# Top-k attention and two gated layers on one core: a lighter decode of layer 2's weights, new latencies in the planner, and zeros multiplied in TensorE's gaps

## The chip, the cores and the metric

The kernel runs on one core of a Trainium2 chip. The metric is device time in microseconds, from a run's start to its end; lower is better. The core has five engines that run side by side, each through its own instructions in a fixed order: TensorE (PE in the profile; PEld is its weight load), VectorE (DVE), ScalarE (ACT), GpSimd (POOL) and SyncE (SP), which here issues all transfers. Engines wait for each other by semaphores.

## The reference

```
scores = q @ k.T / sqrt(64)              # 4 batches, 8 heads, 576 rows, 64 wide
keep the 32 largest scores of a row, softmax over them
x   = attn @ v                           # 2304 tokens x 512
xn  = x / rms(x) * rms_g                 # layer 1, d_ff 1536
x   = (silu(xn @ w_gate) * (xn @ w_val)) @ w_out
out = (sigmoid(x @ w_gate2) * (x @ w_val2)) @ w_out2     # layer 2
```

The weights come in as 64-bit floats, so each value is a pair of 32-bit words (lo, hi), and the kernel turns the pair into a 32-bit float itself.

## The kernel before

The work is cut into 18 units of 128 tokens. Attention runs per unit and head: TensorE makes the scores `sp` in PSUM (two buffers), VectorE finds the 32 largest with four MAX8 and three MATCH_REPLACE8 and masks the exponentials that ScalarE made (`e`), ScalarE and GpSimd split the result into two float16 parts (`ph`), a transposing transfer turns it (`pt`), and TensorE multiplies it with the values (`pv`). Layer 1 of a unit is six products of 48 multiplications (`pg` and `pw` in three blocks) and one of 144 (`py`). Layer 2 is again six products of 48, and 36 wide multiplications (`po`). All products split their operands into two float16 parts.

Both layers' weights are prepared early. Layer 1's nine pieces (w1g, w1v, w1o, three blocks each) stay on chip; layer 2's nine pieces are decoded, scaled, split, written to DRAM (w2g, w2v, w2o) and loaded again as `wl` whenever a batch of units needs them. A piece is four blocks of 128x512. For each block `load_f32` loads the raw words (`raw`, in a ring of seven buffers that `wh` and `wl` share), and makes the float: VectorE shifts and masks the high word into `dec` in PSUM, VectorE joins the sign bits to it, ScalarE scales the low word in place, and GpSimd adds the two. `prep_piece` then finds a power of two that scales the piece, over TensorE and VectorE, and splits the blocks. `consts1` and `consts2` combine all pieces' scales; the first units of layer 1 and of layer 2 wait for them (`c1...`, `c2...`, the latter ending in the tile `c2o`).

Nothing of this is issued as written. `Scheduler` records every operation, gives it a priority (a due place in the order), and `order` walks through a planned time: it picks, again and again, the operation that can start first on some engine, with costs from `cost`. An operation's users become ready at its planned end plus a latency of its engine plus MARGIN; a transfer's users at its planned landing plus a fixed 900 ns. The order that results is the order in which each engine's instructions are written out. Planned times themselves leave no other mark on the program. PSUM tiles tagged `mm` come from one ring of three buffers; `dec`, the scale products, `pg`, `pw`, `py` and `po` share it.

Of the kernel before, what the change touches and what calls it, by code (L numbers as in the profile page):

```python
# [9 lines left out]
F32 = mybir.dt.float32  # L10
F16 = mybir.dt.float16
BF16 = mybir.dt.bfloat16
I32 = mybir.dt.int32
U32 = mybir.dt.uint32
AF = mybir.ActivationFunctionType
ALU = mybir.AluOpType
PSUM = bass.MemoryType.PSUM
DRAM = bass.MemoryType.DRAM
P = 128
# [10 lines left out]

BACKLOG = 8000
COLD = 5000.0
MARGIN = 120

ADDS = (0, 1, 2, 3)
ADDS2 = (0, 1, 2, 3)  # L40
REACH = 100.0
PATIENCE = 0.0

# [90 lines left out]
class Scheduler:  # L134
# [67 lines left out]
    def cost(self, eng, method, args, kw, writes, reads):  # L202

        out = (writes or reads)[0].shadow
        src = max([x.shadow for x in reads] + [out], key=lambda a: math.prod(a.shape[1:]))
        n = math.prod(src.shape[1:])
        psum = any(x.tile.pool.space == PSUM for x in reads + writes)
        ptrs = sum(isinstance(x, _View) for x in (*args[2:], kw.get("scalar"), kw.get("scale"), kw.get("bias")))
        if eng == "tensor":
            rate = 0.6 if method == "matmul" and kw["rhs"].shadow.dtype == F32 else 2.4  # L210
            return math.prod(out.shape[1:]) / rate + 2.7, 260
        if eng == "vector":
            if method in ("max", "match_replace", "tensor_tensor"):
                ptrs = 0
            if method == "match_replace":
                return n / 0.96 + 130, 170
            fast = method in ("tensor_scalar", "tensor_copy", "memset") and not psum
            return (8 if method == "reciprocal" else 1) * n / (1.92 if fast else 0.96) + 69 + 60 * min(ptrs, 1), 170
        if eng == "scalar":
            return n * 0.8333 + (51 if psum else 93) + 93 * (ptrs + ("accum_out" in kw)), 200  # L220
        if eng == "gpsimd":
            if method == "tensor_tensor":
                return (464 if n == 1 else n * (1.88 if mybir.dt.size(out.dtype) == 2 else 2.1) + 149), 150
            return n * 0.833 + (224 if n == 1 else 161), 150

        run = out.shape[-1] * mybir.dt.size(out.dtype)
        size = n * math.prod(out.shape[:1]) * mybir.dt.size(out.dtype)
        if method == "dma_start_transpose":
            return 1275, size / 290
        return (475 if out.shape[0] == 128 else 650), size / (360 if run >= 512 else 180)  # L230

    def order(self):
# [22 lines left out]
        now = dict.fromkeys(self.ENGINES, 0.0)  # L255
        out, dma, sems, cold = [], 0.0, [0.0] * 8, COLD

# [32 lines left out]
            return best  # L290

        behind = sorted(self.ops, key=lambda op: -op.base)
        while len(out) < len(self.ops):

            while behind[-1].end is not None:
                behind.pop()
            best = choose(behind[-1].base + REACH) or choose(math.inf)
            if best is None:
                raise RuntimeError("the schedule is stuck")
            _, at, op = best  # L300
            cost = op.cost
            if op.eng == "tensor":

                cold = COLD if at - now[op.eng] > 2500 else cold
                slow = min(cost, cold / 2)
                cold -= 2 * slow
                cost += slow
            op.start, op.end = at, at + cost
            done = op.end + op.lat + MARGIN
            if op.eng == "sync":  # L310
                move = op.calls[0][0] == "dma_start_transpose"
                begin = max(op.end + (0 if move else 650), dma)
                dma = begin + op.lat
                done = dma + 900
                sems = sems[1:] + [done]
                if move:
                    op.end = begin + 56
            now[op.eng] = op.end
            ready[op.eng].remove(op)
            out.append(op)  # L320
            for t in op.new:
                r = self.rings[t.key]
                r["free"].pop(0)
                r["lanes"][t.lane].remove(t)
            for t in op.tiles:
                t.left -= 1
                t.end = max(t.end, done)
                if not t.left:
                    r = self.rings[t.key]
                    r["free"].append(t.end)  # L330
                    r["free"].sort()

            for u in op.users:
                u.start = max(u.start, op.end + OWN if u.eng == op.eng != "sync" else done)
            for u in op.users + op.later:
                u.waits -= 1
                if not u.waits:
                    ready[u.eng].append(u)
        self.end = max(now.values())
        return out  # L340

    def issue(self):
        with self.tc.manual_schedule():
# [11 lines left out]
def topk_attention_moe_kernel(  # L355
# [17 lines left out]
    nc = E = Scheduler(tc)  # L373
# [8 lines left out]
    CPJ = 512 // P  # L382
    assert (S, D, R, DM) == (576, 64, 64, 512) and F % 512 == 0 and B % 2 == 0

    def pool(name, bufs, **kw):
        return E.pool(ctx.enter_context(tc.tile_pool(name=name, bufs=bufs, **kw)), bufs, **kw)

    const = pool("const", 1)
# [20 lines left out]
    at = pool("at", 2)  # L409
# [3 lines left out]
    htp = pool("htp", 4)  # L413
# [2 lines left out]
    ps_v = pool("ps_v", 1, space=PSUM)  # L416
    ps_m = pool("ps_m", 3, space=PSUM)
    dram = pool("dram", 1, space=DRAM)

    def pow2_scale(m, n, name, pl=None, out=None):  # L420

# [6 lines left out]
        return s.bitcast(F32), i.bitcast(F32)  # L428


    def load_f32(dst, src, on_pool):

        if src.dtype == F32:
            nc.sync.dma_start(dst, src)
            return
        raw = wbig.tile([P, 512, 2], I32, name="raw", tag="w4")
        nc.sync.dma_start(raw.rearrange("p f a -> p (f a)"), src.bitcast(I32))
        lo, hi, d = raw[:, :, 0], raw[:, :, 1], dst.bitcast(I32)

        t = ps_m.tile([P, 512], I32, name="dec", tag="mm", lane="dec")  # L440
        E.claim(dst)
        nc.vector.tensor_scalar(t, hi, 3, 0x3FFFFFF8, op0=ALU.logical_shift_left, op1=ALU.bitwise_and)
        o = d if on_pool else t
        nc.vector.scalar_tensor_tensor(
            out=o, in0=hi, scalar=-0x40000000, in1=t, op0=ALU.bitwise_and, op1=ALU.bitwise_or
        )
        if on_pool:

            nc.scalar.activation(lo, lo.bitcast(U32), AF.Copy, scale=2.0 ** -29)
            nc.gpsimd.tensor_tensor(out=d, in0=d, in1=lo, op=ALU.add)  # L450
            return
        nc.vector.scalar_tensor_tensor(
            out=d.bitcast(U32), in0=lo.bitcast(U32), scalar=29, in1=t.bitcast(U32), op0=ALU.logical_shift_right, op1=ALU.bitwise_or
        )

    def prep_piece(w, kind, j, g, s, i, place, held=None):

# [2 lines left out]
        for c in range(CPJ):  # L462
            r = (c if kind == "in" else j * CPJ + c) * P
            src = w[r : r + P, j * 512 : (j + 1) * 512] if kind == "in" else w[r : r + P, :]
            fs.append((held or place)(c).bitcast(F32))
            load_f32(fs[-1], src, c in (ADDS if held else ADDS2))

        ps = ps_m.tile([P, P], F32, name="wps", tag="mm", lane="wps")
        with E.group():
# [15 lines left out]
        else:  # L485
            nc.vector.tensor_scalar(n, m, state["g2"], 2.0 ** -30, op0=ALU.mult, op1=ALU.max)
        m = n
        pow2_scale(m, 1, "w", out=(s, i))
        sf = s.bitcast(F32)
        if g is not None:  # L490
            sc = tiny.tile([P, NC], F32, name="gsc")
            nc.gpsimd.tensor_scalar(sc, g, sf, None, op0=ALU.mult)
# [30 lines left out]
    def prep1(n, j):  # L523
        w, kind, g = {"g": (w_gate, "in", g_sb), "v": (w_val, "in", g_sb), "o": (w_out, "out", None)}[n]

        t = res[3 * j + "gvo".index(n)]
        if 3 * j + "gvo".index(n) < 3 * NJ - 1:
            held = lambda c: res[3 * j + "gvo".index(n) + 1][:, c]
        else:
            fs = [htp.tile([P, 2, CPJ, P], F16, name="fs", tag="ht2", bufs=6, lane="fs") for _ in range(CPJ)]  # L530
            held = lambda c: fs[c].rearrange("p a m r -> p (a m r)")
        pieces, s, i = lay1[n]
        prep_piece(w, kind, j, g, s[:, j : j + 1], i[:, j : j + 1], lambda c: t[:, c], held)
        pieces.append([t[:, c] for c in range(CPJ)])

    def prep2(n, j):
        w, kind = {"g": (w_gate2, "in"), "v": (w_val2, "in"), "o": (w_out2, "out")}[n]
        pieces, s, i = lay2[n]
        d = dram.tile([CPJ // 2, P, 2048], F16, name=f"w2{n}{j}")
        ts = [wbig.tile([P, 2, 1024], F16, name="wh", tag="w4") for _ in range(CPJ // 2)]  # L540
        prep_piece(w, kind, j, None, s[:, j : j + 1], i[:, j : j + 1], lambda c: ts[c // 2][:, c % 2])
        for a, t in enumerate(ts):
            nc.sync.dma_start(d[a], t.rearrange("p c f -> p (c f)"))
        pieces.append(d)
# [507 lines left out]
```

## Time and profile before

| | |
|---|---|
| median of 3 runs | 1283.01 us (1282.52 to 1285.65) |
| the profiled execution's own time | 1278.91 us |
| its span, first to last instruction | 1277.1 us |
| mean granted TensorE clock | 0.949 |
| busy: PE, DVE, ACT, POOL | 1136.7, 1021.9, 820.5, 844.6 us |

Busy times are sums over the span; one engine's share differs between stretches, so shares are read by stretch. The granted clock is 1.00 at TensorE's full speed. Every instruction carries line L351, the line at which the recorded operations are issued, so rows are told apart by tile names.

### The profile page before, as it was taken

The page shows a single profiled execution, that of the slowest core. Times are in us where ns is not written, and L with a number is a line of the kernel's source. Part 1 is how long each engine was busy: PE and PEld are TensorE (multiplying, and loading weights), DVE is VectorE, ACT ScalarE, POOL GpSimd, SP SyncE. Part 2 cuts the span into 40 slices and gives each one's busy share as a digit, 9 for nine tenths or more (in the row PEclk, how much of TensorE's full clock was granted, in tenths as well). Part 3 has the DMA queues.
Part 4 walks back from the last instruction along what each step waited for, and adds up shares of the span by engine and source line. Part 5 has one row for each costly group of instructions (what it writes and reads, how often), then busy time and mean ns, then how long its engine had stood idle before and what let it go on. Part 6 is the DMA issues. An engine that isn't in the chain of part 4 may idle for free.

```text
span 1277.1 us, 41563 instructions
## 1 busy us (share of the span) xinstructions
PE 1136.7 (89%) x17020; PEld 972.8 (76%) x17020; DVE 1021.9 (80%) x2571; ACT 820.5 (64%) x1428; POOL 844.6 (66%) x966
## 2 busy tenths in 40 slices
PE   3686364699989999999999999998999999999998
PEld 2343263698889879978896999798869978997986
DVE  6999999987888989898888899787689997980001
ACT  6898677666686757676865567566756665652531
POOL 6897889876677647685866577475747674762530
PEclk9699576799989999999999999998999999999999
DMA  8986788799877686688868577867675575765337
GB/s 283 306 253 156 246 231 225 185 282 243 127 171 158 132 185 126 135 187 184 173 140 192 118 172 136 196 127 159 137 183 118 130 168 127 175 147 138 126 106 274
DMA packets 323775, 225.26 MB, mean 176 GB/s; under 512 B 278401, under 2 KB 286593, under 8 KB 323585
## 3 DMA queue, kind: packets, MB, share of 16 engines
q1 hardware_dynamic: 323584, 222.62, 71.5%
q8 instruction: 133, 2.18, 0.7%
q14 instruction: 58, 0.47, 0.1%
HBM read 147.06 MB, written 14.16 MB: 126 GB/s over the span
## 4 chain that ended last, share of the span: by engine, by line
PE 52%; DMA 14%; DVE 8%; POOL 7%; issue 4%; ACT 4%; SPq 1%; POOLq 0%; ACTq 0%; DVEq 0%
PE pw L351 15%; PE pg L351 14%; PE po L351 9%; PE py L351 8%; DMA pt<-ph 7%; PE pv L351 3%; DMA qt<-qn 3%; DVE m L351 3%; PE sp L351 3%; DVE w L351 2%; POOL ph L351 2%; DMA xt<-sn 2%; POOL sg L351 2%; POOL wh L351 1%; SPq L351 1%
## 5 line engine op out<-in xcount | busy, mean ns | idle before, releaser
L351 DVE MAX8 m<-w 128x8 f32<-128x576 f32 x432 | 317.6, 750 | 3.1
L351 PEld LDWEIGHTS <-wl 128*128 128x128 f16 x5184 | 296.2, 99 | 2.3 <-issue 1.6
L351 POOL TENSOR_TENSOR ph<-e,ph 128x512 f16<-128x512 f32 (+1 forms) x288 | 204.5, 734 | 69.6 <-ACT ph L351 68.1
L351 DVE MATCH_REPLACE8 w<-m,w 128x576 f32<-128x576 f32 x288 | 213.3, 743 | 0.0
L351 POOL TENSOR_TENSOR sg<-sg,sv 128x512 f32<-128x512 f32 x105 | 133.9, 1276 | 44.9 <-ACT sv L351 41.1
L351 ACT ACTIVATE e<-sp,nb,sc 128x576 f32<-128x576 f32 x144 | 117.6, 829 | 69.5 <-DVE w L351 25.0
L351 PE MATMUL pg<-xt,w1g 128*128 128x128 f16 x2592 | 157.7, 222 | 4.5 <-DMA xt<-sn 4.5
L351 PE MATMUL pg<-yt,wl 128*128 128x128 f16 x2592 | 157.7, 222 | 0.9 <-POOL yt L351 0.9
L351 PEld LDWEIGHTS <-w1g 128*128 128x128 f16 (+1 forms) x2624 | 153.8, 100 | 5.0 <-issue 4.7
L351 PEld LDWEIGHTS <-w1v 128*128 128x128 f16 (+1 forms) x2640 | 150.7, 99 | 8.5 <-POOL w1v L351 5.4
L351 PE MATMUL pw<-xt,w1v 128*128 128x128 f16 x2592 | 154.7, 220 | 0.1
L351 PEld LDWEIGHTS <-w1o 128*128 128x128 f16 (+1 forms) x2640 | 150.9, 99 | 4.1 <-DVE w1g L351 3.3
L351 PE MATMUL pw<-yt,wl 128*128 128x128 f16 x2592 | 153.5, 219 | 0.4 <-DVE ym L351 0.2
L351 POOL TENSOR_TENSOR ht<-sg,ht 128x512 f16<-128x512 f32 x105 | 122.0, 1162 | 46.9 <-ACT ht L351 44.1
L351 PE MATMUL py<-ht,w1o 128*128 128x128 f16 x2592 | 150.0, 221 | 0.0
L351 PE MATMUL po<-wl,ht 128*128 128x512 f16 x648 | 145.5, 379 | 0.0
L351 DVE MAX8 m<-sp 128x8 f32<-128x576 f32 x144 | 108.2, 759 | 41.5 <-PE sp L351 40.3
L351 ACT ACTIVATE ph<-e 128x576 f16<-128x576 f32 x144 | 97.1, 677 | 51.5 <-DVE e L351 49.2
L351 PE MATMUL pv<-vt,pt 128*128 128x65 f16 (+1 forms) x2240 | 91.5, 198 | 39.8 <-DMA pt<-ph 38.6
L351 PEld LDWEIGHTS <-pt 128*128 128x128 f16 (+1 forms) x2240 | 80.9, 103 | 51.6 <-DMA pt<-ph 45.1
L351 PE MATMUL sp<-kt,qt 128*128 128x512 f16 (+3 forms) x640 | 96.8, 299 | 25.8 <-DVE e L351 13.3
L351 DVE SCALAR_TENSOR_TENSOR e<-sp,m,e 128x576 f32<-128x576 f32 x144 | 115.2, 809 | 3.0 <-ACT e L351 0.2
(164 smaller groups left out, 1763.1 us busy)
## 6 DMA issues: line engine op xcount, KB each, us to landing
wl<-w2g SPq DMA_DIRECT2D x60, 512.0 KB, 4.7
wl<-w2v SPq DMA_DIRECT2D x60, 512.0 KB, 4.8
wl<-w2o SPq DMA_DIRECT2D x60, 512.0 KB, 5.1
raw<-in_moe_w_gate_dram SPq DMA_DIRECT2D x24, 512.0 KB, 4.7
raw<-in_moe_w_val_dram SPq DMA_DIRECT2D x24, 512.0 KB, 5.1
raw<-in_moe_w_out_dram SPq DMA_DIRECT2D x24, 512.0 KB, 5.3
qr<-in_q_dram SPq DMA_DIRECT2D x32, 128.0 KB, 3.6
kr<-in_k_dram SPq DMA_DIRECT2D x16, 256.0 KB, 4.2
```

The costliest lines, as they stand in the source:

```text
L351: getattr(eng, method)(*map(real, a), **{n: real(x) for n, x in k.items()})
```

## The change

Three things change. First, blocks of layer 2's weights are decoded another way (`way` 1 in `load_f32`): ScalarE writes the scaled low word to `dec` in PSUM and the sign of the high word, as 1.0 or -1.0, over the low word in place; VectorE joins the shifted high word and `dec` in one operation; GpSimd adds the two as integers. The scale found for such a piece is then corrected by two additions on a 128x1 column. Layer 1's blocks keep their way (now called 2). Second, the planner's figures: MARGIN goes from 120 to 30 ns, the engines' latencies fall by 20 to 60 ns (ScalarE's stays), a transfer lands 1700 ns instead of 900 after its planned end, and two costs of GpSimd grow. Third, `order` puts an extra operation ahead of a TensorE operation when TensorE's planned time lies between 30 and 300 us and has a gap: as many 128x512 multiplications of a tile of zeros as take 0.6 of the gap at 216 ns each, into a `mm` buffer that is free by the plan. Nothing reads their result.

```diff
-MARGIN = 120
-ADDS = (0, 1, 2, 3)
-ADDS2 = (0, 1, 2, 3)
+IDLE = (30000, 300000)
+FILL = 0.6
+LAND = 1700
+MARGIN = 30
+WAYS = (((2, 2, 2, 2),) * 9, ((1, 1, 1, 1),) * 9)
+HELD2 = False
...
-            return math.prod(out.shape[1:]) / rate + 2.7, 260
+            return math.prod(out.shape[1:]) / rate + 2.7, 200
...
-                return n / 0.96 + 130, 170
+                return n / 0.96 + 130, 150
...
-                return (464 if n == 1 else n * (1.88 if mybir.dt.size(out.dtype) == 2 else 2.1) + 149), 150
-            return n * 0.833 + (224 if n == 1 else 161), 150
+                return (516 if n == 1 else n * (1.88 if mybir.dt.size(out.dtype) == 2 else 2.1) + 149), 100
+            return n * 0.833 + (224 if n == 1 else 161 + 300 * min(ptrs, 1)), 100
...
             cost = op.cost
+            if op.eng == "tensor" and IDLE[0] < now["tensor"] < IDLE[1]:
+                fill = self.idle(at - now["tensor"], now["tensor"])
+                if fill:
+                    now["tensor"] = fill.end
+                    out.append(fill)
...
-                done = dma + 900
+                done = dma + LAND
...
+    def idle(self, gap, now):
+        pool, lhs, rhs = self.spare
+        n = int(FILL * gap / 216)
+        r = self.rings[(id(pool), "mm")]
+        if not n or not r["free"] or r["free"][0] > now:
+            return None
+        r["free"].pop(0)
+        ps = pool.tile([P, 512], F32, name="idle", tag="mm")
+        op = _Op()
+        op.eng, op.new, op.start, op.end = "tensor", [ps.tile], now, now + 216.0 * n
+        op.calls = [("matmul", (ps,), dict(lhsT=lhs, rhs=rhs, start=True, stop=True))] * n
+        r["free"].append(op.end + 150)
+        r["free"].sort()
+        return op
...
+    zeros = const.tile([P, 512], F16, name="zeros")
+    nc.gpsimd.memset(zeros, 0.0)
+    E.spare = (ps_m, zeros[:, 0:P], zeros)
...
+        if way == 1:
+            nc.scalar.activation(t, lo.bitcast(U32), AF.Copy, scale=2.0 ** -29)
+            nc.scalar.activation(lo.bitcast(F32), hi, AF.Sign)
+            nc.vector.scalar_tensor_tensor(out=d, in0=hi, scalar=3, in1=t, op0=ALU.logical_shift_left, op1=ALU.bitwise_or)
+            nc.gpsimd.tensor_tensor(out=d, in0=d, in1=lo, op=ALU.add)
+            return
...
+        if 1 in ways:
+            h = tiny.tile([P, 1], I32, name="ws")
+            pow2_scale(m, 1, "w", out=(h, i))
+            for x, y in ((s, h), (i, i)):
+                nc.vector.tensor_scalar(x, y, (-1.0, 1.0)[x is i] * (1 << 23), None, op0=ALU.add)
+            sf = h.bitcast(F32)
```

## Rows read from the trace of the kernel before

**Rows 1.** The page: busy times, then TensorE and its granted clock in 40 slices.

```profile
PE 1136.7 (89%) x17020; PEld 972.8 (76%) x17020; DVE 1021.9 (80%) x2571; ACT 820.5 (64%) x1428; POOL 844.6 (66%) x966
...
PE   3686364699989999999999999998999999999998
...
PEclk9699576799989999999999999998999999999999
```

**Rows 2.** Windows: length, busy us of each engine (instructions), granted clock, DMA share, GB/s.

```profile
30.00:100.00 70.00, 53.56 (x290) 27.25 (x289) 65.12 (x165) 63.64 (x114) 62.76 (x71) 0.85 0.90 268
100.00:256.00 156.00, 87.48 (x959) 67.44 (x957) 151.03 (x381) 113.14 (x200) 135.61 (x144) 0.72 0.77 214
256.00:400.00 144.00, 133.96 (x2244) 123.63 (x2241) 123.09 (x325) 101.67 (x180) 99.97 (x115) 0.96 0.86 195
400.00:1152.00 752.00, 729.96 (x11844) 648.78 (x11841) 655.36 (x1618) 482.24 (x837) 494.10 (x586) 0.99 0.70 155
1152.00:1277.10 125.10, 121.12 (x1662) 99.62 (x1659) 8.11 (x28) 40.00 (x65) 33.79 (x29) 1.00 0.49 163
```

**Rows 3.** Waits of DVE, 30 to 256 us: total us, times, longest; seven groups.

```profile
DVE dec L351 <- DMA raw<-in_moe_w_out_dram: 2.6, 2, 1.5
...
DVE e L351 <- ACT e L351: 0.2, 1, 0.2
```

**Rows 4.** Tiles dec and c2o: count, duration min/median/max, first and last start.

```profile
L351 DVE SCALAR_TENSOR_TENSOR wh<-raw,dec x36: 666/674/678, 99.8 to 237.8; 128x512 int32<-128x512 int32 x36
...
L351 DVE TENSOR_SCALAR c2o<-c2u x1: 139/139/139, 250.0 to 250.0; 128x1 int32<-128x1 int32 x1
```

**Rows 5.** Groups of instructions: count, busy us, mean ns, idle before; weight preparation.

```profile
L351 DVE TENSOR_SCALAR dec<-raw 128x512 int32<-128x512 int32 x72 | 49.0, 686 | 6.4 <-DMA raw<-in_moe_w_out_dram 2.6 <-DMA raw<-in_moe_w_val_dram 2.6 <-DMA raw<-in_moe_w_gate_dram 0.4
L351 ACT ACTIVATE raw<-raw 128x512 int32<-128x512 uint32 x72 | 46.3, 674 | 16.3 <-DMA raw<-in_moe_w_val_dram 8.6 <-DMA raw<-in_moe_w_gate_dram 5.0 <-DMA raw<-in_moe_w_out_dram 2.5
L351 POOL TENSOR_TENSOR wh<-wh,raw 128x512 int32<-128x512 int32 x36 | 46.2, 1292 | 14.0 <-ACT e L351 3.8 <-DVE wh L351 3.8 <-ACT qr L351 3.1
...
L351 DVE SCALAR_TENSOR_TENSOR wh<-raw,dec 128x512 int32<-128x512 int32 x36 | 24.2, 673 | 0.0
...
L351 ACT ACTIVATE w1v<-wlo 128x512 f16<-128x512 f32 x12 | 7.1, 592 | 5.3 <-PE wlo L351 5.3
...
L351 DVE TENSOR_SCALAR p2t<-wn 128x1 int32<-128x1 int32 x18 | 2.6, 144 | 0.0
```

**Rows 6.** Groups of instructions of one head on VectorE.

```profile
L351 DVE MAX8 m<-w 128x8 f32<-128x576 f32 x432 | 317.6, 750 | 3.1
...
L351 DVE MATCH_REPLACE8 w<-m,w 128x576 f32<-128x576 f32 x288 | 213.3, 743 | 0.0
...
L351 DVE SCALAR_TENSOR_TENSOR e<-sp,m,e 128x576 f32<-128x576 f32 x144 | 115.2, 809 | 3.0 <-ACT e L351 0.2
```

**Rows 7.** The chain that ended last: start us, us, what.

```profile
251.71 4.62 PE pg L351 x48
...
331.59 2.59 PE po L351 x12
...
520.69 8.04 PE py L351 x144
...
556.22 2.68 PE pg L351 x48
```

**Rows 8.** Timeline, 430 to 447 us: start us, us, instruction.

```profile
441.78 0.68 ACT L351 ACTIVATE ph<-e 128x576 f16<-128x576 f32 x1
...
442.54 1.43 POOL L351 TENSOR_TENSOR ph<-e,ph 128x512 f16<-128x512 f32 x2 [0.23 <-ACT ph L351]
```

**Rows 9.** DMA issues: count, median us from issue to landing.

```profile
pt<-ph SPq DMA_TRANSPOSE x144, 4.2
```

**Rows 10.** Waits of PE, 256 to 1152 us: total us, times, longest.

```profile
PE pv L351 <- DMA pt<-ph: 17.8, 24, 1.9
```

**Rows 11.** Groups of instructions: ScalarE's table loads.

```profile
L351 ACT ACT_TABLE_LOAD x1 | 1.3, 1283 | 0.7 <-PEq L1038 0.7
```

More of the change, by code (lines that the diff above doesn't have):

```diff
@@ L215, in cost @@
             if method == "match_replace":
-                return n / 0.96 + 130, 170
+                return n / 0.96 + 130, 150
             fast = method in ("tensor_scalar", "tensor_copy", "memset") and not psum
-            return (8 if method == "reciprocal" else 1) * n / (1.92 if fast else 0.96) + 69 + 60 * min(ptrs, 1), 170
+            return (8 if method == "reciprocal" else 1) * n / (1.92 if fast else 0.96) + 69 + 60 * min(ptrs, 1), 150
         if eng == "scalar":
@@ L292, in order @@
         behind = sorted(self.ops, key=lambda op: -op.base)
-        while len(out) < len(self.ops):
+        left = len(self.ops)
+        while left:
+            left -= 1
             while behind[-1].end is not None:
@@ L428, in pow2_scale, with load_f32 @@
         return s.bitcast(F32), i.bitcast(F32)
-    def load_f32(dst, src, on_pool):
+    def load_f32(dst, src, way):
         if src.dtype == F32:
@@ L441, in load_f32 @@
         E.claim(dst)
+        if way == 1:
[4 more added lines that the diff above has]
+            return
         nc.vector.tensor_scalar(t, hi, 3, 0x3FFFFFF8, op0=ALU.logical_shift_left, op1=ALU.bitwise_and)
-        o = d if on_pool else t
         nc.vector.scalar_tensor_tensor(
-            out=o, in0=hi, scalar=-0x40000000, in1=t, op0=ALU.bitwise_and, op1=ALU.bitwise_or
+            out=d if way == 2 else t, in0=hi, scalar=-0x40000000, in1=t, op0=ALU.bitwise_and, op1=ALU.bitwise_or
         )
-        if on_pool:
+        if way == 2:
             nc.scalar.activation(lo, lo.bitcast(U32), AF.Copy, scale=2.0 ** -29)
@@ L454, in load_f32, with prep_piece @@
         )
-    def prep_piece(w, kind, j, g, s, i, place, held=None):
+    def prep_piece(w, kind, j, g, s, i, place, held, ways):
         fs = []
@@ L465, in prep_piece @@
             fs.append((held or place)(c).bitcast(F32))
-            load_f32(fs[-1], src, c in (ADDS if held else ADDS2))
+            load_f32(fs[-1], src, ways[c])
         ps = ps_m.tile([P, P], F32, name="wps", tag="mm", lane="wps")
@@ L487, in prep_piece @@
         m = n
-        pow2_scale(m, 1, "w", out=(s, i))
-        sf = s.bitcast(F32)
+        if 1 in ways:
[4 more added lines that the diff above has]
+            sf = h.bitcast(F32)
+        else:
+            pow2_scale(m, 1, "w", out=(s, i))
+            sf = s.bitcast(F32)
         if g is not None:
@@ L532, in prep1 @@
         pieces, s, i = lay1[n]
-        prep_piece(w, kind, j, g, s[:, j : j + 1], i[:, j : j + 1], lambda c: t[:, c], held)
+        prep_piece(w, kind, j, g, s[:, j : j + 1], i[:, j : j + 1], lambda c: t[:, c], held, WAYS[0][len(pieces)])
         pieces.append([t[:, c] for c in range(CPJ)])
@@ L540, in prep2 @@
         ts = [wbig.tile([P, 2, 1024], F16, name="wh", tag="w4") for _ in range(CPJ // 2)]
-        prep_piece(w, kind, j, None, s[:, j : j + 1], i[:, j : j + 1], lambda c: ts[c // 2][:, c % 2])
+        held = None
+        if HELD2:
+            fs = [htp.tile([P, 2, CPJ, P], F16, name="fs", tag="ht2", bufs=6, lane="fs") for _ in range(CPJ)]
+            held = lambda c: fs[c].rearrange("p a m r -> p (a m r)")
+        prep_piece(w, kind, j, None, s[:, j : j + 1], i[:, j : j + 1], lambda c: ts[c // 2][:, c % 2], held, WAYS[1][len(pieces)])
         for a, t in enumerate(ts):
```

## The prediction, made before the changed kernel was run

> **What bounds the kernel now.** I read the page's busy times and slices first [rows 1]. TensorE is busy for 89% of the span, but the slices show two regimes: 3 to 7 tenths over much of the first 256 us, with a granted clock of 5 to 7 tenths in several slices, then 9 almost to the end. So I cut the span into stretches [rows 2]. From 256 us on TensorE works 985.0 of 1021.1 us (96.5%), and VectorE is behind it (655.4 of 752 us from 400 to 1152, 8.1 of the last 125). Before 256 us it is the reverse: from 100 to 256 us VectorE works 151.0 of 156 us (96.8%) and TensorE 87.5, so TensorE is idle for 68.5 us, at a mean clock of 0.72. ScalarE (113.1) and GpSimd (135.6) have some room there, GpSimd little. VectorE's waits from 30 to 256 us are seven groups of 9.1 us in all, the longest for a load of raw weights; none is for scores [rows 3].
>
> What ends the first regime: layer 2's weights are decoded from 99.8 to 237.8 us, and the constants that open layer 2 come at 250.0 us [rows 4]. From then on TensorE has work for every idle moment. So a microsecond is won early if the stretch before 250 us gets shorter, or if TensorE gets more of its work done inside it; and later only if TensorE's own stalls (32.1 us from 256 to 1152) change.
>
> **The change part by part.**
>
> *Decode of layer 2's weights.* 36 blocks lose VectorE's first operation (dec<-raw, 686 ns): 24.7 us. Nine pieces gain two small operations on a 128x1 column; the nearest row is 144 ns, so 18 x 0.144 = 2.6 us. VectorE: -22.1 us. ScalarE gains 36 Sign operations that read and write the strided raw words; the row of the same shape is raw<-raw, 674 ns: +24.3 us. ScalarE's other operation, now raw<-raw, will write PSUM; no row shows that, the nearest rows lie between 592 and 674 ns [rows 5], so I leave it at 674 (592 would give 3 us back). GpSimd's add and VectorE's remaining operation are the same instructions as before. GpSimd also clears one 128x512 tile at the start, where the first loads hide it.
>
> Does ScalarE pay what VectorE saves? By rows the two operations cost the same, 674 and 686 ns. The Trainium skill (ScalarE: Activation LUTs, Rules for kernel authors) speaks against such a move: it sends element-wise work to VectorE, which it calls up to about three times faster in bf16. By that rule I would estimate the 36 operations at 74 us on ScalarE; this trace, with 32-bit strided words, does not bear it out, and I keep 24.3.
>
> The sum for the stretch from 100 to 256 us: VectorE 151.0 - 22.1 = 128.9, ScalarE 113.1 + 24.3 = 137.4, GpSimd 135.6 as before. VectorE is no longer the fullest. What comes of it can take two ways. (i) The stretch shrinks until ScalarE is as full as VectorE was: 137.4 / 0.968 = 142 us, 14 us less. (ii) The pieces keep their pace (each piece needs its raw loads, GpSimd's 4 x 1.29 us and a free buffer, not only VectorE), and VectorE uses the 22.1 us for attention. A head costs it four MAX8, three MATCH_REPLACE8 and one scalar_tensor_tensor, 6.0 us [rows 6]: 3.7 heads, 0.46 of a unit of eight. One unit's first layer is 6 x 2.68 + 8.04 = 24.1 us of TensorE [rows 7], so 11.1 us of it moves into TensorE's idle 68.5 us and is missing from the later regime. The bounds are 0 (the freed time is idle) and 22.1 (all of it comes back). Three engines at 83 to 88% that work in a fixed order seldom pack to 97%, so I take the lower route, rounded down: 10 us.
>
> *The planner's latencies.* The planner now allows less time per handover, margin included: VectorE 290 to 180 ns, ScalarE 320 to 230, GpSimd 270 to 130, TensorE 380 to 230. A transfer's landing allowance grows from 900 to 1700 ns. Planned times set only the order, so the question is whether the plan comes nearer to the chip. For ph from ScalarE to GpSimd the plan had 573 + 320 = 893 ns and now has 803; the trace has 0.68 us and a gap of 0.08, 760 [rows 8]. For the transpose of ph the plan had 1275 + 1017 + 900 = 3.19 us and now has 3.99; the trace's median from issue to landing is 4.2 [rows 9]. Both come nearer, neither is past it by more than 0.2 us. Where TensorE waits in the later regime, the largest group is pv for that very transpose: 24 times, 17.8 us, 0.74 us each [rows 10]. From VectorE's e to pv the plan loses 110 + 90 + 140 ns and gains 800, so pv is placed 0.46 us later: up to 24 x 0.46 = 11.0 us of TensorE come back. Against it, everything else that TensorE waits for is planned 90 to 150 ns earlier, and some of it will be late instead. Bounds: 11 won, 9 lost (half of the present 17.8 again); I take 4 won. The corrected GpSimd costs touch early operations that TensorE waits for while it is not the bound: nothing.
>
> *Zeros on TensorE.* TensorE is idle 16.4 us from 30 to 100 us and 68.5 from 100 to 256 [rows 2]. The planner fills 0.6 of each gap it sees, at most 51 us: about 236 multiplications at 216 ns (twelve of the same size took 2.59 us at full clock [rows 7]), fewer where no buffer is free or the gap is short. What they buy: real work at the full clock. Before 250 us TensorE's speed hides behind VectorE, which waits for it hardly at all [rows 3]; on the path are the first products after the constants (48 in 4.62 us against 2.68 [rows 7]), some 2 us. What they cost: at the lower of the clock's two levels (1.2 of 2.4 GHz) the same count lasts 1.2 of its gap, 0.2 of the gap too long, and takes one of three PSUM buffers that the decode shares. A late score is hidden by the second score buffer, a head's 6.0 us. With that cover gone it would be 0.2 x 84.9 = 17 us. I take nothing, between 3 won and 5 lost.
>
> *Sum.* Against the profiled execution: 1278.9 - 10 - 4 = 1264.9 us. The timed runs' median of 1283.0 lies 4.1 us above that execution, so I forecast 1269 us.
>
> **The rivals.**
> *More comes back:* the stretch shrinks and attention is ahead too, all 22.1 us and some 6 us of pv's stalls: 1283 - 28 = 1255. For it: VectorE's waits are few, so it can use every freed microsecond. Against: GpSimd is already 87% full.
> *The decode is not what holds layer 2 back:* the constants stay near 250 us because raw loads, GpSimd and buffers set the pieces' pace (156 us for nine, 17 each, of which VectorE's part is 4 x 1.36 us), and VectorE's freed time goes idle for want of buffers. Gain 0 to 4: 1281.
> *Slower, the plan is too tight:* with 40 ns of slack in place of 130 on the handover shown, a small delay blocks TensorE in its fixed order. A unit has some 32 groups on TensorE, 16 units lie in the stretch: about 510 groups. If one in four blocks it 0.2 us longer, 25 us are lost; with the early 10 won, 1298, and with one in eight no change. It decides once TensorE's idle time from 256 to 1152 us passes 32.1 + 10 + 4 = 46 us. Against it: both shown plan times stay near the trace.
> *The zeros get in the way:* the whole overrun of 17 us reaches VectorE, less 10 won: 1290. It decides when VectorE's wait for scores before 256 us, none now, passes 14 us.
> *Sign does not share a table with the others:* the trace has one table load of 1283 ns for Exp, Tanh, Square and Copy together [rows 11]; whether Sign joins them no row shows. If not, up to 72 loads are 92 us on ScalarE: (137.4 + 92) / 0.968 = 237 us for the stretch, some 1360 in all. The Trainium skill (ScalarE: Activation LUTs, Table sets: the hidden batching unit) says that cheap functions stand in every set as filler, which speaks against this rival, and puts a switch at about 2.66 us; an estimate by that is 192 us.
>
> **How the numbers follow.** Forecast 0.50 (its own range 1258 to 1277: early 5 to 16, stalls 0 to 8, zeros 3 either way), more comes back 0.15, decode not the holder 0.13, too tight 0.12, zeros in the way 0.07, tables 0.03. This kernel's runs cannot tell less than 0.3% (3.9 us) from no change. Faster: 0.15 + 0.48 of the forecast + 0.02 of the third = 0.65; within 0.3%: 0.02 + 0.11 + 0.01 = 0.14; slower: 0.21. The range 1250 to 1291 leaves out the tables, the worse part of too tight, and a gain beyond 33 us.
>
> **What would show it.** Right: dec's count on VectorE falls from 72 to 36, with 36 more ScalarE operations near 0.67 us; the constants c2o before 245 us, or attention further on at that time; TensorE's clock near 1.0 from 30 to 256 us with some 200 operations of 216 ns; pv's wait for pt under 12 us. Wrong: c2o still at 250 us and VectorE idle before it; more than one table load; TensorE idle over 46 us from 256 to 1152; a wait of VectorE for scores before 256 us.

## The result and the profile after

The changed kernel takes 1268.54 us (median of 4 runs, 1261.47 to 1269.91) against 1282.76 for the kernel before; the ratio is 0.9877 with a 95% interval of [0.9834, 0.992]. Six further runs gave 1266.22 us and 0.9869 [0.9839, 0.9899]. The profiled execution shown here is the quickest of the first four, 1261.47 us with a span of 1259.6.

The page of the changed kernel, the lines that answer to [rows 1]:

```profile
PE 1152.3 (91%) x17164; PEld 969.6 (77%) x17164; DVE 1002.2 (80%) x2553; ACT 837.6 (66%) x1464; POOL 844.4 (67%) x967
...
PE   3787677798999999999999999999999999999998
...
PEclk9898997899999999999999999999999999999999
```

Its windows, with the columns of [rows 2]:

```profile
30.00:100.00 70.00, 54.29 (x303) 27.48 (x303) 68.79 (x180) 66.72 (x123) 64.77 (x73) 0.90 0.91 284
100.00:256.00 156.00, 116.46 (x1248) 79.47 (x1247) 137.37 (x372) 133.14 (x237) 137.61 (x147) 0.89 0.81 213
256.00:400.00 144.00, 135.25 (x2336) 123.81 (x2334) 124.44 (x331) 103.22 (x183) 103.98 (x119) 1.00 0.89 212
400.00:1152.00 752.00, 732.37 (x11725) 643.37 (x11723) 645.17 (x1595) 480.12 (x833) 490.42 (x580) 1.00 0.71 155
1152.00:1259.60 107.60, 102.74 (x1521) 89.42 (x1517) 7.13 (x24) 34.84 (x56) 27.98 (x23) 0.99 0.45 160
```

After 256 us the kernel before needed 1021.1 us, with TensorE busy for 985.0 of them; now it is 1003.6, with 970.4 busy. So of the 17.5 us that these two executions lie apart, 14.6 are busy time of TensorE and 2.9 idle time (36.1 to 33.2). The busy time fell for two reasons. After 256 us TensorE has 166 instructions fewer (15742 before, 15576 now); at the mean of 62.6 ns for one that is some 10 us, an estimate. The rest fits the granted clock, which rose from 0.96 to 1.00 between 256 and 400 us and from 0.99 to 1.00 after that. In the profiled execution of the six further runs (1267.09 us), in the same order, TensorE is busy 976.5 us after 256 us and idle 32.7, so several of the 17.5 us belong to this one quick execution. VectorE's busy time from 100 to 256 us fell from 151.0 to 137.4 us. TensorE's clock there rose from 0.72 to 0.89.

Decode and constants in the changed kernel (tiles dec and c2o, as [rows 4]), and the zeros:

```profile
L380 ACT ACTIVATE dec<-raw x36: 605/628/665, 93.0 to 242.1; 128x512 int32<-128x512 uint32 x36
L380 DVE SCALAR_TENSOR_TENSOR wh<-raw,dec x36: 664/679/689, 94.7 to 242.8; 128x512 int32<-128x512 int32 x36
...
L380 DVE TENSOR_SCALAR c2o<-c2u x1: 141/141/141, 256.8 to 256.8; 128x1 int32<-128x1 int32 x1
...
L380 PE MATMUL idle<-zeros x144: 376/379/634, 38.2 to 270.0; 128*128 128x512 f16 x144
```

ScalarE's operations on the raw words by shape (the first row is the new Sign, the second layer 1's scaling, as before), and its table loads, which answer to [rows 5] and [rows 11]:

```profile
L380 ACT ACTIVATE raw<-raw 128x512 f32<-128x512 int32 x36 | 24.1, 676 | 0.3
L380 ACT ACTIVATE raw<-raw 128x512 int32<-128x512 uint32 x36 | 23.2, 679 | 2.8 <-DMA raw<-in_moe_w_val_dram 2.4 <-DMA raw<-in_moe_w_gate_dram 0.4
...
L380 ACT ACT_TABLE_LOAD x1 | 1.3, 1283 | 0.7 <-PEq L1090 0.7
```

The constants of layer 2 come later than before (256.8 against 250.0 us), not earlier. What moved ahead is the other work. Layer 1's gate products (`pg`, first line of each pair) and value products (`pw`, second line) before 256 us, first in the kernel before, then in the changed one. The first busy time is PE's, with the multiplications in brackets; the others are those of the engines that read the products:

```profile
0.00:256.00 256.00, 15.25 (x190) 3.94 (x6) 0.79 0.82 236
0.00:256.00 256.00, 8.54 (x144) 0.00 (x0) 2.03 (x3) 0.79 0.82 236
```

```profile
0.00:256.00 256.00, 14.23 (x240) 5.28 (x8) 0.91 0.84 238
0.00:256.00 256.00, 14.98 (x228) 0.00 (x0) 2.79 (x4) 0.91 0.84 238
```

334 multiplications became 468. The heads that VectorE had begun by 256 us (the first MAX8 of each), in the kernel before and in the changed one:

```profile
L351 DVE MAX8 m<-sp 128x8 f32<-128x576 f32 x22 | 16.6, 756 | 1.3 <-PE sp L351 1.3
```

```profile
L380 DVE MAX8 m<-sp 128x8 f32<-128x576 f32 x24 | 18.1, 756 | 3.1 <-PE sp L380 3.1
```

VectorE's waits from 30 to 256 us in the changed kernel, the two longest groups, which answer to [rows 3]:

```profile
DVE wh L380 <- ACT dec L380: 9.0, 7, 5.0
DVE m L380 <- PE sp L380: 3.1, 1, 3.1
```

Part of what the decode freed on VectorE turned into a new wait: for ScalarE, which now has to deliver `dec` first, 9.0 us in seven waits, one of them 5.0 us long. And TensorE's largest wait from 256 to 1152 us, which answers to [rows 10]:

```profile
PE pv L380 <- DMA pt<-ph: 12.7, 18, 1.6
```

It was 17.8 us before. In the profile of the six further runs it is 10.3 us in 16 waits.

### The profile page after: what moved, and what is told of

It is laid out like the page before. It is cut to its first block, busy times and chain, and to the rows that moved or that the text cites. A ratio compares the mean times of both kernels' runs of the same rounds, so it can differ in the third digit from the quotient of the medians.

```text
span 1259.6 us, 41878 instructions
## 1 busy us (share of the span) xinstructions
PE 1152.3 (91%) x17164; PEld 969.6 (77%) x17164; DVE 1002.2 (80%) x2553; ACT 837.6 (66%) x1464; POOL 844.4 (67%) x967
## 4 chain that ended last, share of the span: by engine, by line
PE 36%; DVE 17%; POOL 13%; DMA 12%; ACT 12%; issue 7%; SPq 2%; POOLq 0%; ACTq 0%; DVEq 0%
PE pg L380 10%; PE pw L380 10%; DVE m L380 7%; PE po L380 7%; DMA pt<-ph 6%; DVE w L380 6%; PE py L380 5%; POOL ph L380 4%; POOL sg L380 3%; PE sp L380 2%; PE pv L380 2%; POOL ht L380 2%; DVE e L380 2%; ACT e L380 2%; SPq L380 2%
## 5 line engine op out<-in xcount | busy, mean ns | idle before, releaser
L380 PE MATMUL pg<-xt,w1g 128*128 128x128 f16 x2592 | 153.6, 219 | 5.3 <-DMA xt<-sn 3.3
L380 PEld LDWEIGHTS <-w1g 128*128 128x128 f16 (+1 forms) x2624 | 148.6, 98 | 8.3 <-DMA xt<-sn 4.4
L380 ACT ACTIVATE ht<-sg 128x512 f16<-128x512 f32 x105 | 65.8, 627 | 75.8 <-POOL sg L380 75.6
L380 PEld LDWEIGHTS <-ht 128*128 128x128 f16 x648 | 61.2, 98 | 68.1
```

Of the source, the lines that this page charges most:

```text
L380: getattr(eng, method)(*map(real, a), **{n: real(x) for n, x in k.items()})
```

## The experiments

All ratios are to the kernel before, timed on the same chip. Each profile is of one execution, which may lie some us off the median of its kernel; where that bears on a reading, the text says so.

**The changed kernel's order with the zeros not issued.** The order of every other instruction is that of the changed kernel on all five engines. The zeros feed no output.

```diff
             for op in self.order():
+                if op.new and op.new[0].args[2].startswith("idle"):
+                    continue
```

> The changed kernel in its own order on every engine, with the 144 multiplications of zeros left out of the program. It tells what the zeros do as work from what they do to the order. If the zeros buy nothing, as the prediction had it: within 4 us of the changed kernel (1265 to 1272). If their gain is the clock (the mean granted clock rose from 0.72 to 0.89 between 100 and 256 us, from 0.949 to 0.979 in all): the clock falls back to about 0.95 and the time rises by the 10 to 15 us that TensorE's real work then lasts longer, to about 1280. If they stand in the way, the time falls by up to 5 us.

Measured: 1264.88 us, ratio 0.9863 [0.9842, 0.9885], against 0.9877 and 0.9869 with the zeros issued. From 100 to 256 us:

```profile
100.00:256.00 156.00, 92.44 (x1092) 74.12 (x1091) 135.99 (x368) 130.75 (x233) 135.75 (x144) 0.70 0.78 210
```

The clock is back at 0.70 and TensorE's busy time 24.0 us lower, and the time is the same. So what the clock that the zeros hold up gives in this stretch, and what their work costs, come together to nothing that can be measured. This run does not price the two apart. It fits that TensorE is not what the stretch waits for: it is idle 63.6 of the 156 us, and VectorE's wait for scores before 256 us is 4.7 us here and 3.1 with the zeros. After 256 us the clock is 1.00 up to 400 us here too, so that rise is not owed to the zeros.

**The changed kernel planned without zeros.**

```diff
-IDLE = (30000, 300000)
+IDLE = (0, 0)
```

> The changed kernel with the planner's gap filling off, so that the rest of the order is planned without it. If the zeros buy nothing: 1265 to 1272. If they pay by the clock: about 1280, as with the zeros left out of the program. If the order around them is what counts, this one and the one with the zeros left out differ by more than 4 us.

Measured: 1258.74 us, 0.9805 [0.9784, 0.9827]; the quickest of all kernels run, and clear of the changed kernel. It differs from the run above in the order and in the clearing of one tile at the start, and by 0.6%. So what tells the two apart is the order that the planner wrote, not the zeros' work. VectorE's wait for `dec`, 9.0 us in the changed kernel, is 0.3 us here.

**The changed kernel with the old decode.**

```diff
-WAYS = (((2, 2, 2, 2),) * 9, ((1, 1, 1, 1),) * 9)
+WAYS = (((2, 2, 2, 2),) * 9, ((2, 2, 2, 2),) * 9)
```

> The changed kernel with the decode of layer 2's weights as before (two VectorE operations per block, 22 us more VectorE work before 256 us). By the prediction the decode is worth 10 us: about 1279. If the zeros or the latencies made the gain, it stays at 1265 to 1272. In the changed kernel VectorE was idle 18.6 of the 156 us from 100 to 256 us, so most of the freed time may have gone unused; then the loss is under 5 us.

Measured: 1274.41 us, 0.9943 [0.9923, 0.9963]: 0.7% above the changed kernel by the ratios, 6 to 8 us by the medians. So much of the gain goes with the decode.

**The kernel before with the new decode alone.** The diff is that of the decode in the change; MARGIN, latencies and landing are as before, no zeros.

> The kernel before with the new decode alone: old latencies, no zeros. By the prediction 10 us less than before, about 1273. If the freed VectorE time goes idle (constants of layer 2 at 256.8 us in the changed kernel, later than the 250.0 before), 1279 to 1283.

Measured: 1274.15 us, 0.9932 [0.9912, 0.9953], 8.7 us of 1283. Constants, and layer 1's two groups before 256 us, in its profile:

```profile
L380 DVE TENSOR_SCALAR c2o<-c2u x1: 140/140/140, 261.4 to 261.4; 128x1 int32<-128x1 int32 x1
```

```profile
0.00:256.00 256.00, 18.20 (x240) 6.33 (x10) 0.80 0.84 238
0.00:256.00 256.00, 14.21 (x240) 0.00 (x0) 3.23 (x5) 0.80 0.84 238
```

The constants are 11 us later than before, and 480 multiplications of layer 1 are done in place of 334. At 2.68 us for 48 [rows 7] the 146 are 8.2 us of TensorE's work, about what the median gained. The profile does not show that they made the gain. It is the slowest of the six executions (1277.43 us), with a span only 1.4 us shorter than that of the kernel before: after 256 us TensorE is busy 7.8 us less there and idle 6.3 us more (42.4).

**The planner's figures alone**: MARGIN, landing, all latencies and the two GpSimd costs of the change; old decode, no zeros.

```diff
-MARGIN = 120
+MARGIN = 30
-        ... rate + 2.7, 260
+        ... rate + 2.7, 200
...
-                done = dma + 900
+                done = dma + 1700
```

> The kernel before with the planner's new figures alone (MARGIN, engine latencies, GpSimd costs, landing 1700 ns): old decode, no zeros. The prediction gave them 4 us: 1279. From the runs so far, decode alone gives 8 us and decode with the new figures 24, so if the parts add up the figures are worth some 15 us: about 1267.

Measured: 1279.27 us, 0.9967 [0.9943, 0.9991]. That is the size that the prediction gave, 4 us, but the wait that should have paid for it did not fall. It was 17.8 us in the kernel before, and here it is:

```profile
PE pv L380 <- DMA pt<-ph: 19.1, 20, 4.7
```

This execution took 1283.61 us, 4.3 above its kernel's median. By 256 us it has done 489 multiplications of layer 1's two groups, more than any kernel with the new decode, though it has the old one and has begun 22 heads, as before. So that count alone does not price a kernel. The next three experiments take the figures apart.

**The landing allowance alone**, 900 to 1700 ns.

```diff
-                done = dma + 900
+                done = dma + 1700
```

> The kernel before with the landing allowance of 1700 ns alone. If what the figures win is TensorE's wait for the transpose of ph (17.8 us in the later regime), nearly all of their gain is here: as the run with all figures, and that wait is under 10 us. If it is the shorter handovers, 1280 to 1285.

Measured: 1262.77 us, 0.9851 [0.9816, 0.9887]: 19 us from one constant. pv's wait from 256 to 1152 us, and the windows of the same stretch:

```profile
PE pv L380 <- DMA pt<-ph: 6.7, 8, 1.6
```

```profile
256.00:1152.00 896.00, 871.88 (x14144) 774.58 (x14143) 773.48 (x1941) 588.04 (x1024) 603.26 (x707) 0.99 0.74 165
```

The wait falls by 11.1 us. TensorE's idle time in the stretch falls from 32.1 to 24.1 us. The constant is used for every transfer, not for the transposes alone, so other waits and the order before 256 us move with it.

**The shorter handovers alone**: MARGIN, all latencies and the two GpSimd costs of the change, landing at 900.

```diff
-MARGIN = 120
+MARGIN = 30
-        ... rate + 2.7, 260
+        ... rate + 2.7, 200
...
```

> The kernel before with the shorter handovers and the GpSimd costs alone: landing 900 ns, old decode, no zeros. All figures together won 0.3%, landing alone 1.5%; so if parts add up the handovers lose 1.2%: about 15 us slower than before, with pv's wait above 17.8 us and TensorE idle over 45 us after 256 us. If the shorter handovers are only another order among many, within 5 us of before.

Measured: 1287.27 us, 1.0036 [1.0017, 1.0055]: slower by 4.6 us, where the sum of parts asked for 15. By what was set down, a change within 5 us can also be only another order; the wait and TensorE's idle time rose as the sum of parts had it.

```profile
PE pv L380 <- DMA pt<-ph: 25.6, 25, 2.9
```

```profile
256.00:1152.00 896.00, 852.01 (x13851) 760.01 (x13849) 776.24 (x1930) 577.94 (x1003) 586.88 (x692) 0.99 0.71 159
```

pv now waits 25.6 us. Worked out afterwards: the chain from VectorE's `e` to the transfer is planned 0.34 us shorter, and 24 times 0.34 is 8.2: 17.8 + 8.2 = 26.0. TensorE is idle 44.0 us in the stretch, 11.9 more than before.

**The landing allowance doubled in its step**, 2500 ns.

```diff
-                done = dma + 900
+                done = dma + 2500
```

> The kernel before with the landing allowance at 2500 ns, twice the step. If the gain of landing is that pv is placed later and its wait goes: pv's wait falls further, from 17.8 by 6.7 to under 4 us, and the time is no worse than with 1700 (ratio 0.985 or below). If 1700 was a lucky order, the ratio goes back to 0.99 to 1.00 though the wait falls.

Measured: 1266.76 us, 0.9872 [0.9851, 0.9893]. The time is near the 0.985 asked for, not below it, and the wait did not fall under 4 us:

```profile
PE pv L380 <- DMA pt<-ph: 7.6, 5, 3.7
```

So more allowance does not take away what was left at 1700. That two values win 1.3 and 1.5% speaks against luck at 1700, and so does every other pair of runs that differ in the allowance alone: with the shorter handovers the ratio goes from 1.0036 to 0.9967, with the new decode from 0.9932 to 0.983.

**The zeros alone**: the kernel before with the gap filling and nothing else of the change.

```diff
+            if op.eng == "tensor" and IDLE[0] < now["tensor"] < IDLE[1]:
+                fill = self.idle(at - now["tensor"], now["tensor"])
...
```

> The kernel before with the zeros alone. If they cost time as in the changed kernel (where the kernel planned without them is about 10 us faster): 1286 to 1293. If that cost belonged to that one order: 1280 to 1285. If a warm clock pays: below 1279.

Measured: 1281.24 us, 0.9984 [0.9961, 1.0006], no change that can be told.

**Landing and decode, nothing else.** The diffs of the two.

> The kernel before with the landing allowance and the new decode, and nothing else: old handover latencies, no zeros. Landing alone gave 1.5%, the decode alone 0.7%. If they add up: a ratio of 0.978, 1.2% less than the changed kernel. If the decode needs the shorter handovers (with them it gave 1.6%), it stays near landing alone, 0.985. If the two win the same idle time of TensorE: 0.985 too, with pv's wait as low as with landing alone (6.7 us).

Measured: 1262.09 us, 0.983 [0.9805, 0.9856]. The decode adds 0.2% to landing's gain, inside the intervals; pv's wait is 13.7 us. They do not add up.

**A neighbouring order**: the changed kernel without zeros, MARGIN 60 in place of 30.

```diff
-MARGIN = 30
+MARGIN = 60
```

> The changed kernel without zeros, with MARGIN at 60 in place of 30: a neighbouring order, the same work. It tells how far two orders of one work lie apart. If the order's chance is worth under 4 us: 0.978 to 0.983. If it is of the size of the zeros' cost (8 us): anywhere from 0.975 to 0.988.

Measured: 1271.95 us, 0.9914 [0.9883, 0.9944]: 1.1% more than with 30, with the same instructions. The windows from 256 to 288 us, with 30 and then with 60:

```profile
256.00:288.00 32.00, 31.11 (x555) 30.10 (x553) 29.28 (x70) 23.32 (x41) 26.84 (x31) 1.00 1.13 295
```

```profile
256.00:288.00 32.00, 20.65 (x310) 18.54 (x311) 29.38 (x76) 20.47 (x34) 24.08 (x29) 0.84 0.78 198
```

In these 32 us TensorE is busy 10.5 us less. The constants of layer 2 come at 265.1 us with 60 and at 250.5 with 30. The profile with 60 is the slowest of its six executions (1279.45 us).

## Why the prediction was right

*The time.* 1269 was forecast; 1268.5 and 1266.2 were measured. The forecast's parts were 10 for the decode, 4 for the figures and 0 for the zeros; alone they measure 8.7, 4.2 and 2.0, the last not to be told from none. The sum of these, 14.9 us, is close to the 14.2 of the first runs. That it is this close is partly luck: two orders of the same work lay 1.1% apart in the last experiment, which is nearly the whole gain, and inside the two larger parts the working was wrong, as follows. (The spans of the terms as the prediction lists them would give 1256 to 1281, wider than the 1258 to 1277 written there; nothing else hangs on that.)

*The signs.* Met: VectorE's `dec` operations fell from 72 to 36, ScalarE has 36 more of 676 ns, there is one table load, attention is two heads further on, and TensorE is idle 28.4 us from 256 to 1152, far from the 46 that would have spoken for a plan too tight. Not met: the constants came at 256.8 us, not before 245; the clock and the number of zeros stayed lower than said; pv's wait was 12.7 us, 10.3 in the repeat, where under 12 was asked. Two signs of being wrong came in part: VectorE was idle 18.6 us from 100 to 256 with the constants no earlier, and it waited once for scores, 3.1 us (1.5 in the repeat), much less than the 14 at which the rival on zeros would have decided.

*The zeros, nothing.* Alone and within the changed kernel's order they change no time that can be told, as taken. What they would show was put too high: 144 multiplications in place of some 200, and a clock of 0.89 to 0.90 from 30 to 256 us, not near 1.0.

*The decode, right in its second way, in part.* Of the two ways in the prediction, the stretch did not shrink: the constants came 7 to 11 us later. VectorE's time went into attention, as (ii) said, but about half of it: its busy time before 256 us fell from 235.3 to 225.4 us in the changed kernel, so of the 22.1 us freed some 12 were used, which is the two heads more at 6.0 us. The forecast had 3.7 heads. The other 10 us went idle, so the rival that the freed time goes unused was half true. In layer 1's two groups 134 multiplications moved ahead in the changed kernel, 7.5 us of TensorE, and 146 with the decode alone, 8.2, where 11.1 was worked out; but the figures alone moved 155 without freeing any of VectorE's time, so that this work is the decode's is argued and not shown. What the runs show is that the time follows the decode, by an amount that depends on the rest of the order: 0.7% alone, 0.7% with figures and zeros, 1.6% with the figures, 0.2%, inside the intervals, with the landing alone.

What holds VectorE back in the changed kernel is seen: it waited 9.0 us for ScalarE's `dec`, 7.6 in the kernel with the decode alone. The prediction had counted ScalarE's new load (24.3 us for the sign, which measures 24.1; 22.5 for `dec`), but not that VectorE is now queued behind ScalarE at every block, with attention behind it in the fixed order. A better order avoids most of that wait: it is 0.3 us in the kernel planned without zeros.

*The figures, right in sum and wrong inside.* "I take 4 won" for all figures together stands against 4.2, but the parts were mis-sized: the landing alone wins 19 us and the handovers alone lose 4.6. The bound of 11.0 us for pv's wait stood for all figures together, which place pv 0.46 us later; with them alone the wait did not fall, and in the changed kernel it fell by 5.1 us. The landing alone places pv 0.80 us later and took 11.1 us off; that this number meets the bound is chance. The landing wins more than this wait, so other things moved too: TensorE's busy time after 256 us fell from 985.0 to 975.1. Only 70 instructions fewer fall there, some 4 us by the mean of 62.6 ns; the rest fits the granted clock, 0.98 in place of 0.96 from 256 to 400 us and 1.00 in place of 0.99 after that. The rival "the plan is too tight" showed in two runs: from 256 to 1152 us TensorE's idle time rose to 44.0 us with the handovers alone and to 42.3 with all figures alone, near the 46 at which that rival would have decided. In the changed kernel it was 28.4. Why all figures without the new decode bring pv's wait back to 19.1 us, though the arithmetic of the plan has pv 0.46 us later, was not settled.

*The tables.* One load of 1283 ns, as before: Sign needed no load of its own.

*What stays open.* The kernel planned without zeros is 0.7% quicker than the changed one. The work of the zeros is not the reason, the order is. But a neighbouring MARGIN moves the same program by 1.1%, so it cannot be said that planning with zeros makes orders worse; it made this one no better. For the neighbour the profile shows the place: the constants of layer 2 arrive 14.6 us later, and TensorE stands idle right after 256 us. With the landing alone the constants come at 262.7 us and the time is still good, so this one moment does not rank the orders by itself.

## What to carry to other kernels

Where a planner writes the order, compare its allowances with the trace kind by kind: one that was 1 us short of what the transfers take (planned 3.19, traced 4.2) won as much alone, once corrected, as the whole change, while shortening the others without it cost time. Work moved from a full engine to one with room still ties the two together: count the waits of the first for the second, not only the busy sums, and do not book all the freed time as used. And before crediting a few tenths of a per cent to an edit that reorders the program, run a neighbour of it; here two orders of the same work lay 1.1% apart.

## What the runs showed of the hardware

ScalarE's conversion of the strided low words takes 628 ns when it writes PSUM, and 674 (kernel before) to 679 (changed kernel) when it writes them back in place, at the same stride. Destination and stride change together, so which of the two makes the difference is not shown. From 100 to 256 us TensorE's granted clock follows the zeros, 0.70 without and 0.89 with them in the same order, and the time does not; TensorE is idle for 63.6 of those 156 us without them, so in that stretch the clock is a symptom. One build spreads by 0.5 to 1.0% from run to run (1254.8 to 1261.7 us for the quickest kernel, 1266.2 to 1279.5 for its neighbour with MARGIN 60), so single profiles of two kernels may lie several us apart without any cause in the program.
